# Chunk 0's four first-layer blocks in one piece, and raw weights loaded behind a read: one reordering at the start of a spectral network

## The chip, the cores and the metric

The kernel runs on one core of a Trainium2 chip. Its engines are PE (TensorE, with PEld for its weight loads), DVE (VectorE), ACT (ScalarE), POOL (GpSimd) and SP (SyncE, which here only issues DMAs). Each engine runs its own instructions strictly in order and waits on semaphores for the others. The metric is the device time of one execution in microseconds, the median of several runs.

## The reference

`x` has 4096 rows of 640 columns, everything in float32. A modulation vector made from `c` gives six vectors of 640.

```python
mod = (_silu(c) @ w_mod).reshape(c.shape[0], 6, 1, -1)      # sa, ca, ga, sb, cb, gb
h = _layernorm(x, axis=-1) * (1 + ca) + sa
x = x + ga * _A_ref(h, A_w1, A_b1, A_w2, A_b2)              # first network
h = _layernorm(x, axis=-1) * (1 + cb) + sb
x = x + gb * _B_ref(h, B_w_gate, B_w_up, B_w_down)          # second network (gated, 1728 wide)
```

The first network takes a real Fourier transform over the 4096 rows, cuts the 640 columns into 4 blocks of 160, and runs on each a two-layer complex network:

```python
hr = zr @ w1[0] - zi @ w1[1] + b1[0];  hi = zi @ w1[0] + zr @ w1[1] + b1[1]   # then relu
or_ = hr @ w2[0] - hi @ w2[1] + b2[0]; oi_ = hi @ w2[0] + hr @ w2[1] + b2[1]
```

The results are shrunk towards zero by 0.01 and transformed back.

## The kernel before

Products keep float32 precision by splitting: a value is rounded to a short format (its high part), and the rest (its low part) is a second operand, so that most products are made of three matmuls. `weights_high` and `weights_low` (L279, L285) do so for the weights: `w1a`, `w1b`, `w1c` of the first layer and `w2a`, `w2b`, `w2c` of the second. High parts are made on ACT or POOL (L283, L281), low parts on DVE (L286).

**The transform's first half.** `x` lies in SBUF as 8 tiles `xa`, tile 0 to 7. Each is normalised, multiplied by `fa` (L421, and for tiles 6 and 7 L437 in another cut of columns), copied back by ACT or DVE (`evac_c`, L449, L447), and written to DRAM, `s1`, by `write_s1` (L351, L354), in three parts `f`. Part 0 holds the frequencies that chunks 0 and 1 need. For tiles 6 and 7 part 0 is written in two pieces, named by their columns: `first` (0 to 127 and 512 to 639) and `rest` (128 to 511).

**Chunks.** There are 8 chunks of 256 frequencies. `load_g` (L310) reads a chunk's rows back from `s1` as tile `g`; chunk 0 comes in two halves, and the second half by `first` and `rest` again. `stage_b(ch, t)` (L613) is the transform's second half for one of five column tiles: t = 0 to 3 hold 128 columns of each block, and t = 4 the last 32 of all four. `evac_b` (L620 ACT, L621 DVE) makes `z` from t < 4. For t = 4 of chunk 0, `evac_r(0, b)` (L643 ACT, L653 DVE) makes the part `rz` of block b straight from PSUM. For every later chunk, `rem_high` and `rem_low` (L663 ACT, L667 DVE) make `rt`, `rem_move` (L676) writes it to DRAM (`rzd`), and `rem_read` (L682) reads it back rearranged as `rz`. For chunk 1 both are issued on POOL's queue, for later chunks on SP's.

**Blocks.** `stage_l1(ch, b)` (L708) is the first layer of one block: 21 matmuls on `z` and `rz`, three PSUM tiles `pl`, then `h` (L725, L726 ACT, L727 DVE) and `u` (L736 ACT, L737 DVE). `tail_l1` (L744 ACT, L745 DVE) makes `r` from `u`. `stage_l2(ch, b)` (L765) is the second layer: 16 matmuls on `h` and `r`, and an addition into `tt` (L767 DVE). A PSUM tile of the first two kinds of `pl` has two buffers, so a block's products wait for the `h` of the block before.

**Order.** It is written out by hand. A loop over positions p = 4 ch + b issues the first layer of block p, the `stage_b` that later positions need, the second layer of block p - 1, and the shrinking and back transform of older blocks. `idle(n)` puts n small products whose result nobody reads. On SP's queue all DMAs go out in the written order, and one that waits holds those behind it.

Of the kernel before, what the change touches and what calls it, by code (L numbers as in the profile page):

```python
# [171 lines left out]
def body(tc, x, w1, b1, w2, b2, wg, wu, wd, c, wm, k_fa, k_tb, k_tx, k_bm, k_bx, k_ga, k_ge, k_id, out, dbg=None):  # L172
    nc = tc.nc
    pe, act, dve, pool = nc.tensor, nc.scalar, nc.vector, nc.gpsimd
# [27 lines left out]
    with ExitStack() as top:  # L202
# [34 lines left out]
        with ExitStack() as af:  # L237
# [11 lines left out]
            def load_weights(pl, w, nm):  # L249
                rm = pl.tile([P, 2, NB, BS], F32, tag="rm", name=f"rm{nm}")  # L250
                rr = pl.tile([P, 2, NB, BS], F32, tag="rr", name=f"rr{nm}")
                nc.sync.dma_start(rm, w[0])
                nc.sync.dma_start(rr, w[1])
                return rm, rr
# [24 lines left out]
            def weights_high(w, h, l, v, sg, eng=None):  # L279
                if eng:  # L280
                    eng.tensor_scalar(w[:, :, h], v, sg, None, op0=OP.mult)  # L281
                else:
                    act.activation(w[:, :, h], v, AF.Copy if isinstance(sg, float) else AF.Identity, scale=sg)  # L283

            def weights_low(w, h, l, v, sg):  # L285
                dve.scalar_tensor_tensor(w[:, :, l], v, sg, f32(w[:, :, h]), op0=OP.mult, op1=OP.subtract)  # L286
# [15 lines left out]
            def load_g(ch, lo=0, hi=32, dma=None, cols=(slice(0, D),)):  # L302
                if ch < 4:
                    src = s1[ch // 2].rearrange("(c q j) n d -> c q n j d", c=2, q=4)[ch % 2]
                else:
                    src = s1[2].rearrange("(c q j f) n d -> f c q n j d", c=2, q=4, f=2)[ch // 2 - 2, ch % 2]
                if lo == 0:
                    gs[ch] = fx.tile([P, 4, D], F32, tag="gx", bufs=2, name=f"g{ch}")
                for e in cols:
                    (dma or nc.sync).dma_start(gs[ch][4 * lo:4 * hi, :, e], src[:, lo:hi, :, e].rearrange("q n j d -> n q j d"))  # L310
# [14 lines left out]
            def idle(n):  # L325
                pz = ps.tile([P, P], F32, tag="p2", name="pz")
                for _ in range(n):
                    mm(pz, ones, ones, start=True, stop=True)
# [4 lines left out]
            with tc.tile_pool(name="sp", bufs=1) as sp:  # L333
# [14 lines left out]
                def write_s1(t, f, cols=None, dma=None):  # L348
                    r = slice((0, 2, 1)[f], 128, (4, 4, 2)[f])
                    if t < 6:  # L350
                        (dma or nc.sync).dma_start(s1[f][:, 4 * t:4 * t + 4, :], xas[t][r])  # L351
                        return
                    for e in cols or (slice(0, 512), slice(512, 640)):
                        (dma or nc.sync).dma_start(s1[f][:, 4 * t:4 * t + 4, e], rst[t][r] if e.start == 512 else xas[t][r, :, e])  # L354
# [85 lines left out]
                def evac_c(t, i, eng=None):  # L440
                    if i == 4:
                        o = rst[t] = low_p.tile([P, 4, 128], F32, tag="e", bufs=2, name=f"rst{t}")
                    else:
                        o = xas[t][:, :, 128 * i:128 * i + 128]
                    v = pas[t, i].rearrange("p (a e) -> p a e", a=4)
                    if eng:
                        eng.tensor_copy(o, v)  # L447
                    else:
                        act.activation(o, v, AF.Copy)  # L449
# [23 lines left out]
                rest = (slice(128, 512),)  # L473
                write_s1(6, 0, first)
                write_s1(7, 0, first)
                load_g(0, 16, 32, None, first)
                for q in ((6, 2), (6, 3), (7, 1), (7, 2), (7, 3)):
                    dft_c(*q)
                jobs = prep_weights(raws[1], w1a, w1b, w1c, True)
# [2 lines left out]
                    weights_high(*job)  # L482
                evac_c(6, 2)
                evac_c(6, 3)
                evac_c(7, 1)
                for job in jobs[3:6]:
                    weights_high(*job)
# [1 line left out]
                evac_c(7, 3)  # L489
                for job in jobs[6:]:  # L490
                    weights_high(*job)
                write_s1(6, 0, rest)
                write_s1(7, 0, rest)
                raws[2] = load_weights(rp, w2, "2")
                load_g(0, 16, 32, None, rest)
                for t in (2, 3):
                    for f in (1, 2):
                        write_s1(t, f)
# [1 line left out]
                first_scale(3, 5)  # L500
                remainders(acc0, wx0)
                pm1 = columns(acc0, wx0)
                idle(8)
                for job in jobs[:4]:
                    weights_low(*job)
                dve.tensor_scalar(ca1, pm1[:, 0:5], 1.0, None, op0=OP.add)
# [26 lines left out]
            w2c = p2.tile([P, NB, 640], F32R, name="w2c")  # L533
            prep2 = prep_weights(raws[2], w2a, w2b, w2c, False)
            prep2 = [prep2[k] for k in (0, 3, 1, 4, 2, 5)]
            for n, job in enumerate(prep2):
                if n // 2 != 1:
                    weights_high(*job, pool)
            pool.dma_start(bm.rearrange("p a b c -> p (a b c)"), k_bm)


# [65 lines left out]
            def stage_b(ch, t):  # L607
                g, tb = gs[ch], tbs[ch]
                pb = (ps.tile([P, 2, 256], F32, tag="p2", name=f"pb{ch}_{t}") if (ch, t) in ((0, 1), (0, 3)) else
                      bank0(1 if t == 4 else 0, [P, 2, 256], f"pb{ch}_{t}"))  # L610
                col = slice(128 * t, 128 * t + 128)
                for j in range(4):
                    mm(pb[:, :, 64 * j:64 * j + 64], g[:, j, col], tb[:, j, :], start=True, stop=True)  # L613
                pbs[ch, t] = pb

            def evac_b(ch, t):
                pb = pbs[ch, t]
                z = lp.tile([P, 2, 2, 258], F32R, tag="z", bufs=4, name=f"z{ch}_{t}")
                zs[ch, t] = z
                act.activation(z[:, 0, :, 0:256], pb, AF.Identity, scale=ca1[:, t:t + 1])  # L620
                dve.scalar_tensor_tensor(z[:, 1, :, 0:256], pb, ca1[:, t:t + 1],  # L621
                                         f32(z[:, 0, :, 0:256]), op0=OP.mult, op1=OP.subtract)
                if ch == CE:
                    pool.tensor_copy(z[:, 0, :, 0:257:256], f32(edge[:, 0, t]))
                    pool.tensor_copy(z[:, 1, :, 0:257:256], f32(edge[:, 1, t]))
                    pool.tensor_copy(z[:, :, :, 257], zero[:, 0, 0])


            def evac_r(ch, b, part=None):
                if part != 1:  # L630
                    evac_rh(ch, b)
                if part != 0:
                    evac_rl(ch, b)
# [246 lines left out]
            for p in range(LAST + 1):  # L880
                ch, b = p // 4, p % 4
                on(shrink, p - 6)
                on(stage_l1, p)

                if p < 2:
                    todo = ([(0, 1), (0, 2)], [(0, 3), (1, 4), (1, 0)])[p]
                elif b == 0:
                    todo = [(ch, 3)]
                else:
                    todo = [(ch + 1, 4)] * (b == 1) + [(ch + 1, b - 1)]  # L890
                todo = [q for q in todo if q[0] < NCH]
                for q in todo:
                    stage_b(*q)
                    if q[1] < 4:
                        evac_b(*q)
                        if q[0] == 0:
                            evac_r(*q)
                for f, *a in sums.get(p, ()):
                    f(*a)
                if p == 0:  # L900
                    for job in prep2[2:4]:
                        weights_high(*job)

                if p == 1:
                    for job in prep2[3:]:
                        weights_low(*job)
                if b == 1 and ch + 1 < NCH:
                    rem_high(ch + 1)
                on(tail_l1, p)
                on(shrink_high, p - 6)  # L910
                if b == 1 and ch + 1 < NCH:
                    rem_low(ch + 1)
                    rem_move(ch + 1)
                if b == 2 and ch + 1 < NCH:
                    rem_read(ch + 1)
                on(stage_l2, p - 1)
                on(stage_i, p - 7)
                on(shrink_low, p - 6)
                if p < LAST:
                    on(shrink_parts, p - 5)  # L920
                if b == 0 and ch:
                    for i in range(4):
                        move_x(ch - 1, i)
                if p == 0:
                    for job in prep2[:3]:
                        weights_low(*job)
                if b == 3 and 2 < ch + 2 < NCH:
                    load_g(ch + 2)
                    load_tb(ch + 2)
                for f, *a in mods.get(p, ()):  # L930
                    f(*a)
                if p == LAST - 4:
                    cf += [rp.tile([P, 2, D], F32, tag=tag, name=f"cf{tag}") for tag in ("rm", "rr")]
                    load_first_rows(rb + 16, rl, nc.sync)
                elif p == LAST - 1:
                    load_first_rows(0, rb - 16, nc.sync)
# [1544 lines left out]
```

## Time and profile before

| what | value |
|---|---|
| median of 3 runs | 1466.28 us (1464.79 to 1469.08) |
| the profiled execution | 1463.59 us |
| its span, first to last instruction | 1461.8 us |
| granted TensorE clock, mean | 0.994 |
| busy: PE, PEld | 1411.0 (97%), 1333.6 (91%) us |
| busy: DVE, ACT, POOL | 1086.9 (74%), 783.2 (54%), 550.3 (38%) us |
| DMA | 380.05 MB, mean 260 GB/s |

A row of the timeline gives the start in us, the length, engine, line and operation, what it writes and reads, the shape and how many instructions it merges; in brackets stand the idle time of the engine just ahead of it and what ended that. A row on SPq or POOLq is the issue of a DMA, not its transfer. PE makes one float32 product in several passes, so a row can count more than the program has. The first products on `z` start near 54 us; the change lies between 46 and 98 us.

### The profile page before, as it was taken

The page shows a single profiled execution, that of the slowest core. Times are in us where ns is not written, and L with a number is a line of the kernel's source. Part 1 is how long each engine was busy: PE and PEld are TensorE (multiplying, and loading weights), DVE is VectorE, ACT ScalarE, POOL GpSimd, SP SyncE. Part 2 cuts the span into 40 slices and gives each one's busy share as a digit, 9 for nine tenths or more (in the row PEclk, how much of TensorE's full clock was granted, in tenths as well). Part 3 has the DMA queues.
Part 4 walks back from the last instruction along what each step waited for, and adds up shares of the span by engine and source line. Part 5 has one row for each costly group of instructions (what it writes and reads, how often), then busy time and mean ns, then how long its engine had stood idle before and what let it go on. Part 6 is the DMA issues. An engine that isn't in the chain of part 4 may idle for free.

```text
span 1461.8 us, 23933 instructions
## 1 busy us (share of the span) xinstructions
PE 1411.0 (97%) x8520; PEld 1333.6 (91%) x8520; DVE 1086.9 (74%) x1967; ACT 783.2 (54%) x1552; POOL 550.3 (38%) x645
## 2 busy tenths in 40 slices
PE   7789999988999999999999999999999999999998
PEld 2589999966888888899999999999999999999998
DVE  8748777867887798757887768787747767567775
ACT  7748888744544555545565546555425445245432
POOL 5300100044563454313445424444324545146533
PEclk9989999999999999999999999999999999999999
DMA  9877767638767988798977998877696666966552
GB/s 376 308 240 226 237 192 226 220 120 280 254 233 250 369 298 265 273 369 307 324 262 250 347 358 265 307 245 254 228 343 219 229 207 240 358 206 240 204 183 88
DMA packets 186474, 380.05 MB, mean 260 GB/s; under 512 B 22227, under 2 KB 104083, under 8 KB 184563
## 3 DMA queue, kind: packets, MB, share of 16 engines
q1 hardware_dynamic: 177826, 361.09, 71.9%
q0 software_dynamic: 6944, 14.82, 3.4%
q10 hardware_dynamic: 1584, 2.62, 0.5%
q8 instruction: 67, 1.10, 0.3%
q14 instruction: 53, 0.43, 0.1%
HBM read 263.91 MB, written 105.39 MB: 253 GB/s over the span
## 4 chain that ended last, share of the span: by engine, by line
PE 60%; DVE 8%; DMA 4%; issue 2%; ACT 1%; POOL 1%; SPq 0%; POOLq 0%; ACTq 0%; DVEq 0%
PE pd L2349 12%; PE pw L2028 8%; PE pw L2030 8%; PE pw L2029 8%; PE pd_X L2209 4%; DMA cr<-s 2%; PE pg L1892 2%; PE pg L1893 2%; PE pg L1894 2%; PE pd_Y L2209 2%; PE pw L2039 2%; PE pw L2040 2%; PE pw L2041 2%; DVE wb L1346 2%; PE pd_Z L2209 1%
## 5 line engine op out<-in xcount | busy, mean ns | idle before, releaser
L2349 PE MATMUL pd<-wdh,a 128*128 128x320 f32 x1040 | 239.2, 310 | 1.5 <-DVE x L2321 0.8
L2349 PEld LDWEIGHTS pd<-wdh,a 128*128 128x128 f32 x1040 | 176.2, 188 | 2.8 <-DVE x L2321 1.0
L1346 DVE TENSOR_TENSOR wb<-r,wb 128x512 fp32r<-128x512 f32 (+3 forms) x156 | 161.1, 1040 | 17.5 <-ACT wb L1343 15.5
L2349 PE MATMUL pd<-wdl,a 128*128 128x320 f32 x540 | 166.2, 309 | 0.0
L2028 PE MATMUL pw<-h,wt 128*128 128x384 f32 x416 | 140.7, 338 | 2.6 <-ACT s_x L2047 1.5
L2030 PE MATMUL pw<-h,wt 128*128 128x384 f32 x416 | 140.0, 337 | 0.0
L2029 PE MATMUL pw<-h,wt 128*128 128x384 f32 x416 | 139.5, 335 | 0.0
L2321 DVE TENSOR_TENSOR x<-x,pd 128x320 f32<-128x320 f32 x240 | 108.7, 477 | 37.7 <-PE pd L2349 34.1
L1343 ACT ACTIVATE wb<-r 128x512 fp32r<-128x512 f32 (+3 forms) x172 | 117.8, 703 | 33.8 <-PE pw L2041 24.3
L2030 PE MATMUL pw<-h,wb 128*128 128x384 f32 x312 | 104.8, 336 | 2.3 <-DVE wb L1346 2.3
L2028 PE MATMUL pw<-h,wb 128*128 128x384 f32 x312 | 105.1, 337 | 0.0
L2029 PE MATMUL pw<-h,wb 128*128 128x384 f32 x312 | 104.6, 335 | 0.0
L1892 PE MATMUL pg<-ht,wb 128*128 128x512 f32 x260 | 103.2, 397 | 1.3 <-ACT wb L1343 1.3
L1894 PE MATMUL pg<-ht,wb 128*128 128x512 f32 x260 | 101.9, 392 | 2.3 <-DVE wb L1346 2.3
L1893 PE MATMUL pg<-ht,wb 128*128 128x512 f32 x260 | 101.9, 392 | 0.0
L2349 PEld LDWEIGHTS pd<-wdl,a 128*128 128x128 f32 x540 | 101.4, 188 | 0.5
L2047 ACT ACTIVATE s_x<-pw 128x384 f32<-128x384 f32 x52 | 25.4, 489 | 114.0 <-PE pw L2030 113.3
L1605 POOL TENSOR_TENSOR cr<-cr,gab 128x640 f32<-128x640 f32 x28 | 47.9, 1710 | 100.9 <-DMA cr<-s 96.3
L2028 PEld LDWEIGHTS pw<-h,wt 128*128 128x128 f32 x416 | 78.1, 188 | 4.5 <-ACT s_x L2047 2.4
L822 POOL DMA_DIRECT2D s<-co x28 | 15.9, 568 | 165.6 <-ACT co L821 157.8
L2029 PEld LDWEIGHTS pw<-h,wt 128*128 128x128 f32 x416 | 78.2, 188 | 0.0
L2030 PEld LDWEIGHTS pw<-h,wt 128*128 128x128 f32 x416 | 78.1, 188 | 0.0
(335 smaller groups left out, 4064.8 us busy)
## 6 DMA issues: line engine op xcount, KB each, us to landing
wt<-td SPq DMA_DIRECT2D x104, 512.0 KB, 5.3
hs<-ho SPq DMA_DIRECT2D x52, 512.0 KB, 5.1
h<-hs SPq DMA_DIRECT2D x32, 768.0 KB, 8.4
r<-in_B_w_gate_dram SPq DMA_DIRECT2D x36, 640.0 KB, 5.0
r<-in_B_w_up_dram SPq DMA_DIRECT2D x36, 640.0 KB, 5.3
wdr<-wdd SPq DMA_DIRECT2D x21, 640.0 KB, 5.2
td<-wt SPq DMA_DIRECT2D x25, 512.0 KB, 5.5
g<-s SPq DMA_DIRECT2D x7, 1280.0 KB, 9.1
```

Source lines behind the costliest of these rows:

```text
L1343: act.activation(wbs[t, n][:, 0, ks, e], raw[t, n][:, ks, e], AF.Copy)
L1346: (pool if onp else dve).tensor_tensor(wbs[t, n][:, 1, ks, e], raw[t, n][:, ks, e], f32(wbs[t, n][:, 0, ks, e]), op=OP.subtract)
L1605: pool.tensor_tensor(crs[r], crs[r], gab, op=OP.mult)
L1892: mm(b, wh, hh, start=(kk == 0), stop=False)
L1893: mm(b, wh, hl, start=False, stop=False)
L1894: mm(b, wl, hh, start=False, stop=(kk == 4))
L2028: mm(b, w(0, kp), a[:, kp, 0], start=start and kp == 0, stop=False, skip_group_check=not start)
L2029: mm(b, w(0, kp), a[:, kp, 1], start=False, stop=False, skip_group_check=not start)
L2030: mm(b, w(1, kp), a[:, kp, 0], start=False, stop=kp == 1, skip_group_check=not start)
L2209: mm(bk[b, i][:, :320], x, y, start=new and j == 0, stop=j == len(seq) - 1, skip_group_check=not new)
L2321: dve.tensor_tensor(x2[:, e], x2[:, e], x[0][:, :320], op=OP.add)
L2349: mm(pd[g, hf][0][:, :320], l, m, start=i == 0, stop=i == len(s) - 1 and not (last and len(gs) > 1))
```

## The change

In the start of chunk 0 the order is changed on every engine; behind it nothing is changed but the numbering of buffers and lines.

- All four first-layer blocks of chunk 0, with the `stage_b` and the tails that they need, stand in one piece at p = 0. Chunk 1's first `stage_b` (t = 4 and 0) and the second layer of block 0 stand behind the fourth block. Before, they stood behind the second block.
- The six low parts of the second layer's weights stand together on DVE behind the fourth block. Before, three stood behind the first block, and three behind the second.
- All six high parts are made on POOL. Before, `w2b` was made on ACT.
- On SP, the `rest` piece of tile 6 goes out ahead of the first read of chunk 0's second half, and the raw weights of the second layer (`rm`, `rr`) behind its second read instead of ahead of it.
- `idle(8)` becomes `idle(6)`.

```diff
                 write_s1(7, 0, first)
-                load_g(0, 16, 32, None, first)
                 for q in ((6, 2), (6, 3), (7, 1), (7, 2), (7, 3)):
                     dft_c(*q)
...
                 evac_c(6, 2)
                 evac_c(6, 3)
+                write_s1(6, 0, rest)
+                load_g(0, 16, 32, None, first)
                 evac_c(7, 1)
...
-                write_s1(6, 0, rest)
                 write_s1(7, 0, rest)
+                load_g(0, 16, 32, None, rest)
                 raws[2] = load_weights(rp, w2, "2")
-                load_g(0, 16, 32, None, rest)
...
-                idle(8)
+                idle(6)
...
-            for n, job in enumerate(prep2):
-                if n // 2 != 1:
-                    weights_high(*job, pool)
+            for job in prep2:
+                weights_high(*job, pool)
...
             for p in range(LAST + 1):
                 ch, b = p // 4, p % 4
                 on(shrink, p - 6)
-                on(stage_l1, p)
-
-                if p < 2:
-                    todo = ([(0, 1), (0, 2)], [(0, 3), (1, 4), (1, 0)])[p]
+                if p > 3:
+                    on(stage_l1, p)
+
+                if p == 0:
+                    for q in range(4):
+                        stage_l1(0, q)
+                        for t in ((1, 2), (3,), (), ())[q]:
+                            stage_b(0, t)
+                            evac_b(0, t)
+                            evac_r(0, t)
+                        tail_l1(0, q)
+                    for job in prep2:
+                        weights_low(*job)
+                    continue
                 elif b == 0:
...
-                        if q[0] == 0:
-                            evac_r(*q)
...
-                if p == 0:
-                    for job in prep2[2:4]:
-                        weights_high(*job)
-
-                if p == 1:
-                    for job in prep2[3:]:
-                        weights_low(*job)
...
-                on(tail_l1, p)
+                if p > 3:
+                    on(tail_l1, p)
...
-                if p == 0:
-                    for job in prep2[:3]:
-                        weights_low(*job)
```

SP's queue around the second half of chunk 0 (`s10` is part 0 of the DRAM array, `xa6` and `xa7` tiles 6 and 7, `g0` chunk 0, `rm2` and `rr2` the raw weights):

```order
 L354 DMA s10<-rst7_511 32x4x128
+L354 DMA s10<-xa6_270 32x4x384
 L310 DMA g0_447<-s10 64x4x128 x2
-L354 DMA s10<-xa6_270 32x4x384
 L354 DMA s10<-xa7_313 32x4x384
-L252 DMA rm2_548<-in_A_w2_dram 128x1280
-L253 DMA rr2_549<-in_A_w2_dram 128x1280
 L310 DMA g0_447<-s10 64x4x384
+L252 DMA rm2_549<-in_A_w2_dram 128x1280
+L253 DMA rr2_550<-in_A_w2_dram 128x1280
 L351 DMA s11<-xa2_124 32x2560
```

One write moved ahead of a read, and two loads of raw weights behind another.

PE before, from the third `stage_b` of chunk 0 (`pb` is named by chunk and t, `pl` and `pc` by chunk, block and part):

```order
L613 MATMUL pb0_3_768<-tb0_401,g0_447 128x2x64 x4
L613 MATMUL pb1_4_780<-tb1_594,g1_592 128x2x64 x4
L613 MATMUL pb1_0_785<-tb1_594,g1_592 128x2x64 x4
L765 MATMUL pc0_0_0_803<-w2a_627,h0_0_0_681 128x320 x3
L765 MATMUL pc0_0_0_803<-w2b_628,h0_0_1_688 128x320 x3
```

PE now, from the end of the fourth block:

```order
L707 MATMUL pl0_3_2_846<-z0_3_768,w1b_93 128x256 x2
L707 MATMUL pl0_3_2_846<-rz0_654,w1c_94 128x256
L612 MATMUL pb1_4_865<-tb1_592,g1_590 128x2x64 x4
L612 MATMUL pb1_0_870<-tb1_592,g1_590 128x2x64 x4
L764 MATMUL pc0_0_0_883<-w2a_625,h0_0_0_681 128x320 x3
```

Chunk 1's two `stage_b` and the second layer's first block moved behind the third and the fourth first-layer block.

DVE before, from the tail of the first block (`r2_0_0` is `r` of chunk 0, block 0; `rt1` the part of chunk 1 that goes through DRAM):

```order
L745 SCALAR_TENSOR_TENSOR r2_0_0_695<-u1_0_0_694,r2_0_0_695 64x256
L286 SCALAR_TENSOR_TENSOR w2a_627<-rm2_548,w2a_627 128x4x160 x2
L286 SCALAR_TENSOR_TENSOR w2b_628<-rm2_548,w2b_628 128x4x160
L727 TENSOR_TENSOR h0_1_0_740<-h32_0_1_0_739,h0_1_0_740 128x256
L727 TENSOR_TENSOR h0_1_1_753<-h32_0_1_1_752,h0_1_1_753 128x256
L737 SCALAR_TENSOR_TENSOR u1_0_1_764<-pl0_1_2_757,b1r_85,u0_0_1_763 64x256
L621 SCALAR_TENSOR_TENSOR z0_3_773<-pb0_3_768,ca1_71,z0_3_773 128x2x256
L653 SCALAR_TENSOR_TENSOR rz0_654<-pb0_4_646,ca1_71,rz0_654 32x256 x2
L621 SCALAR_TENSOR_TENSOR z1_0_790<-pb1_0_785,ca1_71,z1_0_790 128x2x256
L286 SCALAR_TENSOR_TENSOR w2b_628<-rm2_548,w2b_628 128x4x160
L286 SCALAR_TENSOR_TENSOR w2c_629<-rr2_549,sgn_77,w2c_629 128x4x160
L286 SCALAR_TENSOR_TENSOR w2c_629<-rr2_549,w2c_629 128x4x160
```

DVE now, from the tail of the fourth block:

```order
L744 SCALAR_TENSOR_TENSOR r2_0_3_854<-u1_0_3_853,r2_0_3_854 64x256
L286 SCALAR_TENSOR_TENSOR w2a_625<-rm2_549,w2a_625 128x4x160 x2
L286 SCALAR_TENSOR_TENSOR w2b_626<-rm2_549,w2b_626 128x4x160 x2
L286 SCALAR_TENSOR_TENSOR w2c_627<-rr2_550,sgn_77,w2c_627 128x4x160
L286 SCALAR_TENSOR_TENSOR w2c_627<-rr2_550,w2c_627 128x4x160
L620 SCALAR_TENSOR_TENSOR z1_0_875<-pb1_0_870,ca1_71,z1_0_875 128x2x256
L666 SCALAR_TENSOR_TENSOR rt1_878<-pb1_4_865,ca1_71,rt1_878 128x2x256
```

The six low parts are in one piece, behind all four blocks' own work and ahead of chunk 1's.

## The prediction

> **What bounds the kernel now.** I read the page first, then busy time by stage, then the timeline of each engine where TensorE is not full. Times are us from the span's start.
>
> ```profile
> span 1461.8 us, 23933 instructions
> ...
> PE   7789999988999999999999999999999999999998
> ```
>
> ```profile
> 84.00:98.00 14.00, 12.70 (x93) 12.49 (x91) 6.75 (x14) 6.09 (x14) 2.25 (x4) 0.93 0.86 241
> 98.00:200.00 102.00, 101.95 (x795) 101.60 (x796) 77.60 (x147) 83.49 (x172) 9.88 (x28) 1.00 0.70 209
> ```
>
> Columns are the stretch, its length, busy time of PE, PEld, DVE, ACT and POOL, granted clock, DMA share, GB/s. From 98 to 200, PE is busy 101.95 of 102 at clock 1.00: there only its own work sets the pace. The order of every engine behind this place is unchanged. So whatever the edit does must show up as the moment at which PE enters that full stretch, and it is handed to the end one for one: the later thin slices of the page's PE row hold waits between engines that move along with PE. The holes ahead of it are these:
>
> ```profile
> 56.98 0.75 PE L708 MATMUL pl<-rz,w1c 128*128 128x256 f32 x5
> ...
> 61.09 2.87 PE L613 MATMUL pb<-tb,g 128*128 128x128 f32 x16 [3.36 <-DMA g<-s]
> ...
> 73.81 3.76 PE L613 MATMUL pb<-tb,g 128*128 128x128 f32 x16 [5.58 <-DVE rz L653]
> ...
> 87.65 0.68 PE L765 MATMUL pc<-w2a,h 128*128 128x320 f32 x3
> ...
> 90.08 0.52 PE L708 MATMUL pl<-z,w1a 128*128 128x256 f32 x3
> ...
> 92.58 1.06 PE L613 MATMUL pb<-tb,g 128*128 128x128 f32 x8
> 93.39 0.69 PE L765 MATMUL pc<-w2a,h 128*128 128x320 f32 x3
> ...
> 98.05 0.47 PE L708 MATMUL pl<-rz,w1c 128*128 128x256 f32 x2 [1.35 <-DMA rz<-rzd]
> ```
>
> PE waits 3.36 for the second part of `g0`, 5.58 for `evac_r(0, 3)` to free the bank that chunk 1 needs, and 1.35 for `rz` of chunk 1, which goes to DRAM and back. The last of these waits is the door into the full stretch. The rows in between give prices at full clock: a second-layer block takes 90.08 - 87.65 = 2.43, a first-layer block 92.58 - 90.08 = 2.50, a `stage_b` 93.39 - 92.58 = 0.81.
>
> **The second part's read.** On SP, the queue of nearly all loads:
>
> ```profile
> 46.39 0.58 SPq L354 DMA_DIRECT2D s<-rst  x1
> 49.71 1.26 SPq L310 DMA_DIRECT2D g<-s  x2
> 51.06 1.27 SPq L354 DMA_DIRECT2D s<-xa  x2
> 52.39 0.59 SPq L252 DMA_DIRECT2D rm<-in_A_w_dram  x1
> ...
> 54.42 0.58 SPq L310 DMA_DIRECT2D g<-s  x1
> ...
> 58.12 1.17 SPq L310 DMA_DIRECT2D g<-s  x1
> ...
> 68.92 0.31 SPq L515 DMA_DIRECT2D s1h<-g  x1
> ```
>
> ```profile
> g<-s SPq DMA_DIRECT2D x2, 1280.0 KB, 10.3
> ...
> rm<-in_A_w_dram SPq DMA_DIRECT2D x1, 640.0 KB, 4.8
> ...
> rzd<-rt POOLq DMA_DIRECT2D x1, 512.0 KB, 6.8
> rz<-rzd POOLq DMA_DIRECT2D x4, 128.0 KB, 6.0
> s<-xa SPq DMA_DIRECT2D x2, 192.0 KB, 2.6
> ```
>
> The second fence is the table of DMA issues from 36 to 110; its last figure is the median from issue to landing. Tile 6's write fits into SP's free time between 46.97 and 49.71, so the first read stays at 49.71, tile 7's write goes out at 50.97 and lands 2.6 later at 53.6, and the read of columns 128 to 511 is issued at 53.6 instead of 54.42, with no raw weights ahead of it. It now takes 61.09 - 54.42 = 6.67. The ends for the new latency are the 2.6 of the 192 KB writes and that 6.67; between the 192 KB and 640 KB rows, 384 KB interpolate to 3.5, which I take: it lands at 57.1. The first block's products end at 56.98 + 0.75 = 57.73, so the 3.36 goes. What is late next is the evacuation, below.
>
> The raw weights leave 2 later (54.2 against 52.39) and stand behind the read. POOL's work on them:
>
> ```profile
> 57.39 3.71 POOL L281 TENSOR_SCALAR w2a<-rm 128x640 fp32r<-128x640 f32 x2 [16.12 <-PE pl L708]
> ...
> 83.15 0.77 POOL L676 DMA_DIRECT2D rzd<-rt  x1 [12.24 <-DVE tt L767]
> 90.56 2.25 POOL L682 DMA_DIRECT2D rz<-rzd  x4 [6.64 <-PE pc L765]
> ```
>
> The 57.39 is the landing of `rm` (52.39 + 4.8). It becomes about 59.5, and six instructions of 1.9 instead of four end near 71.5. VectorE asks for the last at 76.5 (below), so this is hidden with some 5 to spare. Chunk 1's `g1` landed by 68.92; the stream of loads is held back some 0.9 (SP has nothing to send while it waits for tile 7's write), so 69.8. PE asks for it behind the fourth block, near 70.7 (ACT needs 2 for `h` and `u` of that block, rows below, and ends its `r` at 73.1): hidden, by 1.
>
> **Four blocks in a row.** PE has 2.50 of work per block, but each needs ScalarE:
>
> ```profile
> 59.01 0.38 ACT L736 ACTIVATE u<-pl 64x256 f32<-64x256 f32 x1
> ...
> 67.23 0.40 ACT L744 ACTIVATE r<-u 64x256 fp32r<-64x256 f32 x1
> 67.65 0.47 ACT L725 ACTIVATE h<-pl,b1m 128x256 f32<-128x256 f32 x1
> ...
> 69.25 0.38 ACT L736 ACTIVATE u<-pl 64x256 f32<-64x256 f32 x1
> 69.65 0.69 ACT L620 ACTIVATE z<-pb,ca 128x512 fp32r<-128x512 f32 x1
> 70.36 0.95 ACT L643 ACTIVATE rz<-pb,ca 32x256 fp32r<-32x256 f32 x2
> ```
>
> From `r` at 67.23 to the end of `rz` at 71.31 one block costs ACT 4.08, more than PE's 2.50. ACT is free of the first block at 59.39 and has three blocks and one `r` to go: 59.39 + 3 x 4.08 + 0.42 = 72.05. Waits for VectorE inside (`r` needs its `u`, the second `rz` its predecessor) I put at 1.1: `r` of the fourth block at 73.1, VectorE's half at 73.5. The two `w2b` that ACT loses are work it no longer has.
>
> VectorE's order is shown with the change: all six low parts of the second layer's weights now stand behind the fourth block's `r`, and `z1_0` and `rt1` of chunk 1 behind them; before, three stood behind the first block and three ahead of `rt1`, with two blocks done.
>
> ```profile
> 79.72 0.88 DVE L286 SCALAR_TENSOR_TENSOR w2c<-rr,sgn,w2c 128x640 fp32r<-128x640 f32 x1
> 80.52 0.82 DVE L286 SCALAR_TENSOR_TENSOR w2c<-rr,w2c 128x640 fp32r<-128x640 f32 x1
> ...
> 81.80 0.75 DVE L667 SCALAR_TENSOR_TENSOR rt<-pb,ca,rt 128x512 fp32r<-128x512 f32 x1
> ```
>
> Six at 0.77 from start to start: 73.5 + 4.6 = 78.1, then `z1_0` and `rt1` end at 79.6, against 81.80 + 0.75 = 82.55. That term is **-2.9**. Ends: -4 if ACT never waits, +1 if the second read lands as late as its old latency makes it (60.3 instead of 57.1, so ACT starts 2.1 later) and PE runs cold for the blocks (1.7).
>
> **The door.** `rt1` goes out at 83.15, its reads at 90.56, the product starts at 98.05: 15.5 from the end of `rt1`. By the same rows it would now start at 79.6 + 15.5 = 95.1. PE gets there far sooner: the second layer's first block ends near 80 (`w2c` at 78.1, then half a block), and two `stage_b`, two second-layer blocks and the start of the next take 2 x 0.81 + 2 x 2.43 + 0.7 = 7.2, some 8 with a cold start: 88, against 96.7. So 8 of lead turn into a wait of 7 or more: the holes are not filled but moved to one place. The reads, 7.49 from issue to use, ran partly after the big loads had landed (stretch 84 to 98: DMA share 0.86). Three earlier, they share the engines with `g2` longer. Ends: 0, and (2.25 of issuing + 10.3, the landing of a 1280 KB load) - 7.49 = +5.1. I take **+1.0**, near the first, as POOL's 512 KB write landed in 6.8 in a full stretch.
>
> The Trainium skill, page "DMA: Bandwidth & Descriptors", section "Queues, rings and completion order", says that each DMA engine takes turns between queues packet by packet. By it POOL's reads would not stand behind SP's loads and the 1.0 would go towards 0, the sum to -0.8; the trace agrees so far (6.8 against 10.3).
>
> ```profile
> 74.00:76.00 2.00, 2.00 (x10) 2.00 (x11) 0.00 (x0) 0.00 (x0) 0.00 (x0) 0.50 0.93 339
> 76.00:78.00 2.00, 2.00 (x11) 2.00 (x10) 0.00 (x0) 0.40 (x1) 0.00 (x0) 0.50 1.03 423
> 78.00:80.00 2.00, 1.04 (x5) 0.64 (x4) 1.68 (x3) 1.16 (x3) 0.00 (x0) 0.71 0.99 410
> ```
>
> After the 5.58 wait PE ran at half clock from 73.81 to 78 at least: 4.2 x 0.5 = 2.1 lost, up to 2.7 with the next row. After the 1.35 wait it lost nothing (98 to 200 at 1.00). A wait of 7 puts the door in the first class: **+2.1**.
>
> The Trainium skill, page "TensorE: Matmul & The Clock Gate", Part 1, says that an idle window of about 3.4 us halves the clock until another such window has been busy. By that alone the loss is 1.7, an estimate, and the sum 0.4 lower; the trace agrees with the half.
>
> The two dropped `idle` products end at 52.3 beside the first read's landing (49.71 + 2.6): nothing, at most 0.3.
>
> Sum: -2.9 + 1.0 + 2.1 = +0.2. On the profiled execution (1463.59, the span and 1.8 around it) that is 1463.8; on the median, 2.7 above it, 1466.5. A measurement of this kernel tells about 0.3%, 4.4 us, from no change. The terms' ends give the likeliest case its own range: 1463.5 to 1470.
>
> **Rivals.** *POOL's round trip stretches* (slower). The write and reads of `rz` now lie wholly under SP's writes of tiles 0, 4 to 7 and `g2`. Against: the write's 6.8 in a full stretch. For: loads there land in 10.3. If both took that, 3.5 + 5.1 = 8.6 in place of 1.0; halfway 5.8 gives -2.9 + 5.8 + 2.1 = +5, 1471.5, at the end 1474. It decides once the product that now starts at 98.05 starts later than 100.4 (4.4 - 2.1 = 2.3 later, with the cold clock).
>
> *The round trip shrinks* (faster). With 4.8 of `rm` as landing for write and reads it is 2.0 + 1.2 shorter: -2.9 - 3.2 + 2.1 = -4.0, with an early `rt1` -5.1: 1461. Against it: fewer idle DMA engines than before, not more.
>
> *The edit doesn't do what it says*: the second read lands at 60.3 all the same. Then ACT starts 2.1 later: +2.3, 1468.6, still inside 0.3%.
>
> **How the numbers follow.** Forecast 0.45, the late read 0.12, the stretched trip 0.28, the shrunk trip 0.15. Faster by over 0.3% is the shrunk trip, 0.15; slower the stretched one, 0.28; the rest 0.57. The range from 1461 to 1472.5 cuts about half of the fast case and the upper third of the slow one.
>
> **What would show it.** In the changed profile: no wait of PE on `g` near 58; ACT nearly full from 59 to 73; `rt` ending near 79.6; one wait of PE on `rz` of 6 to 9 with half clock behind it, its product starting near 96. It is wrong if that wait is short or missing, if `rt` ends after 82.5, or if PE is not full from there on.

## The result and the profile after

The changed kernel took 1466.31 us (median of 12 runs, 1461.72 to 1472.49), the kernel before 1465.13 in the same comparison (12 runs, 1460.85 to 1470.58). The ratio is 1.0008, with a 95% interval of 0.9990 to 1.0025: no change that can be told. The forecast was 1466.5, from a median of 1466.28 before (3 runs) and a change of +0.2.

The profiled execution took 1462.63, with a span of 1460.8.

The windows at the door and behind it (columns as in the prediction: stretch, length, busy time of PE, PEld, DVE, ACT and POOL, clock, DMA share, GB/s):

```profile
84.00:98.00 14.00, 6.21 (x44) 6.04 (x43) 3.22 (x6) 0.69 (x1) 2.25 (x4) 0.83 0.84 238
98.00:200.00 102.00, 102.00 (x791) 101.62 (x789) 77.33 (x146) 83.08 (x170) 9.75 (x28) 0.99 0.70 208
```

Of the 14 us ahead of 98, PE was busy in 12.70 before and is busy in 6.21 now. The stretch behind it is as full as it was (102.00 against 101.95). PE's timeline shows where its waits went:

```profile
51.94 2.02 PE L612 MATMUL pb<-tb,g 128*128 128x128 f32 x16 [0.54 <-DMA g<-s]
...
57.62 2.05 PE L612 MATMUL pb<-tb,g 128*128 128x128 f32 x16 [0.36 <-DMA g<-s]
...
75.72 0.41 PE L764 MATMUL pc<-w2a,h 128*128 128x320 f32 x1 [2.74 <-DVE w2a L286]
...
97.28 0.77 PE L707 MATMUL pl<-rz,w1c 128*128 128x256 f32 x2 [7.79 <-DMA rz<-rzd]
...
100.42 1.05 PE L612 MATMUL pb<-tb,g 128*128 128x128 f32 x8
```

The 3.36 on `g` is 0.36, the 5.58 on `rz` of chunk 0 is gone, 2.74 on `w2a` is new, and the 1.35 at the door is 7.79. What feeds the door, from ACT's and DVE's timelines of after (the last row of a block, the first low part, `rt1`):

```profile
73.20 0.42 ACT L743 ACTIVATE r<-u 64x256 fp32r<-64x256 f32 x1 [0.54 <-DVE u L736]
...
74.10 1.56 DVE L286 SCALAR_TENSOR_TENSOR w2a<-rm,w2a 128x640 fp32r<-128x640 f32 x2
...
79.24 0.74 DVE L666 SCALAR_TENSOR_TENSOR rt<-pb,ca,rt 128x512 fp32r<-128x512 f32 x1
```

POOL's timeline (its last work on the raw weights, the write and the reads of the trip):

```profile
68.70 1.81 POOL L281 TENSOR_SCALAR w2c<-rr 128x640 fp32r<-128x640 f32 x1
...
80.29 0.77 POOL L675 DMA_DIRECT2D rzd<-rt  x1 [8.62 <-DVE rt L666]
87.71 2.25 POOL L681 DMA_DIRECT2D rz<-rzd  x4 [6.65 <-PE pc L764]
```

SP's timeline (the second part's read of `g0`, and `g2`):

```profile
53.23 0.55 SPq L310 DMA_DIRECT2D g<-s  x1
...
82.64 1.32 SPq L310 DMA_DIRECT2D g<-s  x1
```

and SP's issue of `g2` in the kernel before:

```profile
82.71 1.26 SPq L310 DMA_DIRECT2D g<-s  x1
```

From the table of DMA issues of after between 36 and 110 (KB each, median us from issue to landing):

```profile
rzd<-rt POOLq DMA_DIRECT2D x1, 512.0 KB, 6.8
rz<-rzd POOLq DMA_DIRECT2D x4, 128.0 KB, 8.0
...
g<-s SPq DMA_DIRECT2D x1, 384.0 KB, 4.4
```

`rt1` ends at 79.98 (82.55 before), so the write leaves 2.86 earlier, and the reads too (87.71 against 90.56). But the reads need 8.0 to land where they needed 6.0, and the product on `rz` starts at 97.28 instead of 98.05. Most of what was won ahead of the door is given back in front of it. SP's issue of `g2`, 1280 KB, did not move (82.64 against 82.71): the reads that leave earlier meet more of it.

In all that follows, **lag** is the time from PE's first `stage_b` of chunk 0 to the first `stage_b` behind the door, chunk 1's third. Here it is 100.42 - 51.94 = 48.48; before it was 99.91 - 52.41 = 47.50, from PE's timeline:

```profile
52.41 2.02 PE L613 MATMUL pb<-tb,g 128*128 128x128 f32 x16
...
99.91 1.05 PE L613 MATMUL pb<-tb,g 128*128 128x128 f32 x8
```

By this the edit cost 0.98. That is read from one profile of each kernel. Three of the runs below (ACT's queue, the filled wait, `g2` behind the reads) have the same order on PE, ACT and DVE up to the end of `rt1` as the changed kernel. From the first `stage_b` to that end the four executions take 27.55, 27.55, 28.00 and 28.04, so a difference of 0.5 between two profiles says nothing. The 0.98 stays put over the full stretch. The same product in PE's timeline of before:

```profile
197.45 1.05 PE L613 MATMUL pb<-tb,g 128*128 128x128 f32 x8
```

and of after:

```profile
197.93 1.05 PE L612 MATMUL pb<-tb,g 128*128 128x128 f32 x8
```

They stand 0.48 apart, and the first `stage_b` stood 0.47 the other way. Behind 280 the two executions drift by some us in either direction, and the span of after ends 1.0 shorter. So single times differ by more than the edit does, and the lag is what the runs below are judged by, with times of several rounds where these exist.

### The profile page after: what moved, and what is told of

The parts are those of the page before. It is cut to its first block, busy times and chain, and to the rows that moved or that the text cites. A ratio compares the mean times of both kernels' runs of the same rounds, so it can differ in the third digit from the quotient of the medians.

```text
span 1460.8 us, 23921 instructions
## 1 busy us (share of the span) xinstructions
PE 1408.0 (96%) x8516; PEld 1331.2 (91%) x8516; DVE 1081.5 (74%) x1967; ACT 782.2 (54%) x1550; POOL 551.3 (38%) x647
## 4 chain that ended last, share of the span: by engine, by line
PE 59%; DVE 8%; DMA 6%; issue 2%; ACT 2%; POOL 1%; SPq 0%; POOLq 0%; ACTq 0%; DVEq 0%
PE pd L2347 12%; PE pw L2026 7%; PE pw L2028 7%; PE pw L2027 7%; PE pd_X L2207 4%; DMA cr<-s 3%; PE pg L1890 2%; PE pg L1891 2%; PE pd_Y L2207 2%; PE pg L1892 2%; PE pw L2037 2%; PE pw L2038 2%; PE pw L2039 2%; DVE wb L1344 2%; PE pd_Z L2207 1%
```

## The experiments

The theory on record for the first runs: the door is the end of `rt1` plus the trip of `rz` to DRAM and back, 15.5 to 17.3, and what stands behind the door is then paid at half clock. What came to it on the way is that the trip is no constant: its reads share the DMA engines with SP's big loads and take longer among them. Against this stand three others: POOL's queue is the slow part, and another queue would do better; the half clock alone explains the loss; the order of the blocks costs PE time by itself.

### Chunk 1's remainder ahead of the low parts

Chunk 1's two `stage_b`, `rt1` and its write stand ahead of the six low parts:

```diff
                         tail_l1(0, q)
+                    stage_b(1, 4)
+                    rem_high(1)
+                    rem_low(1)
+                    rem_move(1)
+                    stage_b(1, 0)
+                    evac_b(1, 0)
                     for job in prep2:
                         weights_low(*job)
```

The same steps at the next block are dropped.

> The changed kernel, but with rt of chunk 1 made and sent off ahead of the six low parts of the second layer's weights. My theory (the door is the end of rt plus the trip through DRAM): rt ends near 75.1 instead of 79.98, the trip takes 15.5 to 17.3, so the first product on rz starts at 90.6 to 92.4 instead of 97.28. TensorE comes there near 90.8 (its second layer waits 1.5 longer for the weights), waits 0 to 1.6 and stays at full clock. Chunk 1's stage_b for t = 3, which stands behind that product and started 47.50 after the first stage_b before and 48.48 after, starts 41 to 42.5 after it. Time near 1460, ratio to before 0.995 to 0.997. Rival (the wait on rz only hides the next one, on weights or evacuation): less than 2 us better than the changed kernel, with another wait of TensorE in its place.

PE's timeline of this run (the wait for the weights, the door's product, the `stage_b` behind it):

```profile
76.73 0.64 PE L764 MATMUL pc<-w2a,h 128*128 128x320 f32 x1 [3.89 <-DVE w2a L286]
...
91.03 0.40 PE L707 MATMUL pl<-rz,w1c 128*128 128x256 f32 x2
...
92.81 1.05 PE L612 MATMUL pb<-tb,g 128*128 128x128 f32 x8
```

POOL's and SP's timelines (write and reads of the trip, then `g2`):

```profile
74.86 0.77 POOL L675 DMA_DIRECT2D rzd<-rt  x1 [2.64 <-DVE rt L666]
81.42 2.24 POOL L681 DMA_DIRECT2D rz<-rzd  x4 [5.80 <-DMA rzd<-rt]
...
83.54 0.85 SPq L310 DMA_DIRECT2D g<-s  x1
```

and the DMA issues (KB each, median us to landing):

```profile
rz<-rzd POOLq DMA_DIRECT2D x4, 128.0 KB, 6.2
```

The reads leave at 81.42, ahead of `g2` at 83.54, and PE does not wait at the door at all: no bracket on the 91.03. The lag is 92.81 - 51.83 = 40.98, 6.5 less than before. One part of the expectation failed: the clock did not stay full. PE waited 3.89 for `w2a`, and ran at half clock from 75.4 to 85.6; even so it reached the door only after `rz` was there. Time: 1461.20 (12 runs) against 1465.53 (17), ratio 0.9968, interval 0.9949 to 0.9987: 4.7 us faster by the ratio. So the trip is what set the door in the changed kernel, and the order of the four blocks is no hindrance.

### ACT's queue for the trip

The change with the write and the reads of chunk 1's `rz` on ACT's queue instead of POOL's:

```diff
-                (pool if ch == 1 else nc.sync).dma_start(rzd[ch, ...
+                (nc.scalar if ch == 1 else nc.sync).dma_start(rzd[ch, ...
```

(and the same for the reads).

> The changed kernel, with the trip of chunk 1's rz (one write, four reads) issued from ScalarE's queue instead of POOL's. If the trip is long because the 16 DMA engines are full of SP's writes and loads, it stays at 15 to 18 from the end of rt to the product, which starts at 95 to 98. If POOL's way of issuing is what is slow, the trip falls to 11 to 13 and the product starts near 92.

ACT's and PE's timelines of this run:

```profile
85.38 0.58 ACTq L675 DMA_DIRECT2D rzd<-rt  x1
86.00 0.69 ACT L619 ACTIVATE z<-pb,ca 128x512 fp32r<-128x512 f32 x1 [11.53 <-DMA s<-xa]
...
98.25 0.56 PE L707 MATMUL pl<-rz,w1c 128*128 128x256 f32 x2 [4.94 <-DMA rz<-rzd]
```

and its DMA issues:

```profile
rz<-rzd ACTq DMA_DIRECT2D x4, 128.0 KB, 2.7
```

`rt1` ended at 79.54, but the write left at 85.38: ACT stood idle for 11.53 until one of SP's DMAs landed, as the profile infers it. So the run tests less than it was meant to. The reads then left at 93.89 and landed in 2.7. The door stands at 98.25 again, with another queue, a write 5 later and reads 6 later: POOL's queue as the cause gets no support, but the queue alone was not isolated. The trip, 18.7, lies outside both of the expected ranges, and the lag is 49.40, more than with the change alone. One time, 1467.19.

### A filled wait

The change with 28 filler products of PE ahead of the door's block:

```diff
+                if p == 4:
+                    idle(28)
                 if p > 3:
                     on(stage_l1, p)
```

> The changed kernel, with 28 small products that nobody reads (about 7 us) ahead of chunk 1's first first-layer block, so that TensorE does not stand idle while rz is on its way. My theory (the wait is the same, but the clock falls in it): the first product on rz still starts near 97.3, the clock stays at 1.00 behind it, and chunk 1's stage_b for t = 3 starts near 47.2 after the first stage_b instead of 48.48, so 1.3 us less. Rival (the clock costs nothing here): no difference within 0.2, or later by what the added products take.

PE's timeline of this run at the door:

```profile
97.81 0.48 PE L707 MATMUL pl<-rz,w1c 128*128 128x256 f32 x2 [1.65 <-DMA rz<-rzd]
...
99.67 1.05 PE L612 MATMUL pb<-tb,g 128*128 128x128 f32 x8
```

The door is where it was, the clock behind it is full, and the lag is 99.67 - 52.87 = 46.80, 1.68 less than with the change alone. Not all of that is the clock: from the door's product to the `stage_b` PE now takes 1.86 instead of 3.14, which is 1.28, and the other 0.4 arose ahead of the door and lies within the scatter of 0.5. So the half clock behind the door costs 1.28 here. It does not explain where the door stands, so it is only a part of the story. One time, 1464.92.

### The parts of the change by themselves

The kernel before with only the moves on SP's queue (the first hunks of the diff), and the change without them:

> The kernel before, with only SP's part of the change (tile 6's write ahead of the first read, raw weights behind the second). My theory: TensorE's wait on g falls from 3.36 to under 1, rt ends 2.5 to 2.9 earlier (near 79.8), the trip takes 15.5 to 17.3, and the wait on rz grows from 1.35 to between 2 and 4. Chunk 1's stage_b for t = 3 starts 45 to 47.5 after the first stage_b instead of 47.50: 0 to 2.5 us gained. Rival (each wait is paid by itself): the whole 3 us are gained and the wait on rz stays near 1.35.

> The changed kernel, with SP's part of the change undone (tile 6's write behind the first read, raw weights ahead of the second; four blocks in one piece). My theory: TensorE waits about 3.4 for g again, ScalarE starts its three blocks 2 to 2.9 later, rt ends near 82 to 83, the trip takes 15.5 to 17.3 and the wait on rz stays near 8 with half clock behind it: chunk 1's stage_b for t = 3 starts 50 to 51.5 after the first stage_b (47.51 before, 48.48 after). Rival (the blocks gain by themselves, and the raw weights' move is what costs): 47.5 or less.

PE's timeline with SP's part alone:

```profile
57.59 2.05 PE L613 MATMUL pb<-tb,g 128*128 128x128 f32 x16 [0.55 <-DMA g<-s]
...
71.13 3.76 PE L613 MATMUL pb<-tb,g 128*128 128x128 f32 x16 [6.61 <-DVE rz L653]
...
96.96 0.47 PE L708 MATMUL pl<-rz,w1c 128*128 128x256 f32 x2 [3.05 <-DMA rz<-rzd]
```

PE's and POOL's timelines with the blocks alone:

```profile
61.02 3.49 PE L612 MATMUL pb<-tb,g 128*128 128x128 f32 x16 [3.70 <-DMA g<-s]
...
97.77 0.77 PE L707 MATMUL pl<-rz,w1c 128*128 128x256 f32 x2 [5.44 <-DMA rz<-rzd]
...
93.04 2.24 POOL L681 DMA_DIRECT2D rz<-rzd  x4 [8.55 <-DMA rzd<-rt]
```

and the DMA issues with the blocks alone:

```profile
rz<-rzd POOLq DMA_DIRECT2D x4, 128.0 KB, 2.9
```

SP's part does what it says: the wait on `g` falls from 3.36 to 0.55, and most of it comes back as 6.61 on `rz` and 3.05 at the door. Lag 47.10, 0.4 less than before, which is too little to tell. The blocks alone give 49.12, 1.6 more than before, and less than the 50 to 51.5 that were expected: the wait at the door was 5.44 instead of about 8, and the trip 14.4, below its range. Over the three kernels `rt1` ended at 79.88, 79.98 and 83.41, but the door stood at 96.96, 97.28 and 97.77. An `rt1` 3.4 later moved it by 0.5: its reads, issued at 93.04, behind the big loads, took 2.9 instead of 8.0. This is what showed that the trip is no constant. The comparison isn't clean, since with the blocks alone SP's loads also ended sooner (`g2` was issued at 81.16, and the DMA share is 0.12 from 92 to 93, against 1.13 after). Times: 1464.96 and 1468.43, one each; the changed kernel's own times spread from 1461.72 to 1472.49, so a single time tells nothing of 2 us.

### The kernel before with `rt1` ahead of its low parts

Three of the low parts at the second block are moved behind `rt1`'s evacuation and write, in the kernel before:

```diff
-                if p == 1:
-                    for job in prep2[3:]:
-                        weights_low(*job)
...
                     rem_move(ch + 1)
+                if p == 1:
+                    for job in prep2[3:]:
+                        weights_low(*job)
```

> The kernel before, with rt of chunk 1 made and sent off ahead of the three low parts that stood in front of it, and nothing else. My theory: rt ends about 2.4 earlier (near 80.1), the trip takes 15.5 to 17.3, rz is there at 95.6 to 97.4, TensorE comes there near 97 as its second layer gets the weights 0.7 later: the wait on rz falls from 1.35 to under 0.7, and chunk 1's stage_b for t = 3 starts 46.7 to 47.4 after the first stage_b instead of 47.51. So on the kernel before this move is worth under 1 us, as TensorE itself is late there. Rival (the trip alone sets the door there too): 45 or less.

PE's timeline of this run, in the second layer's first block:

```profile
81.67 0.63 PE L765 MATMUL pc<-w2b,h 128*128 128x320 f32 x1 [2.87 <-DVE w2b L286]
```

A miss: lag 48.62, more than before. PE waits 2.87, and then 0.63, for the low parts that were moved, runs at half clock from 81.1 to 87.9, and so reaches the door at 98.92, later than the reads (97.16). The wait at the door is gone because PE is late, not because the trip got short. `rt1` itself came 1.7 sooner (80.88), and its reads landed 0.75 sooner. One time, 1463.32.

### The first experiment with fillers

14 fillers behind chunk 1's `evac_b`, so that PE would not lose its clock in the wait of 3.89 on `w2a`:

```diff
                     evac_b(1, 0)
+                    idle(14)
                     for job in prep2:
```

> The first experiment (rt ahead of the six low parts) with 14 small products that nobody reads (3.5 us) between chunk 1's stage_b for t = 0 and the second layer's first block, where TensorE waits 3.9 for the low parts. My theory of the clock: no half clock from 75 to 86 there (10.2 us of it without these products), so TensorE reaches the product on rz 2.5 to 3.5 earlier and now waits for it until about 90; chunk 1's stage_b for t = 3 starts 39 to 40.5 after the first stage_b instead of 40.98. Rival (the clock is not lost through that wait): 40.9 to 41.5.

PE's timeline of this run (the first wait on the low parts, and the door):

```profile
77.31 0.41 PE L764 MATMUL pc<-w2a,h 128*128 128x320 f32 x1 [1.16 <-DVE w2a L286]
...
95.04 0.47 PE L707 MATMUL pl<-rz,w1c 128*128 128x256 f32 x2 [3.47 <-DMA rz<-rzd]
```

POOL's and SP's timelines (the reads, and `g2`):

```profile
83.38 2.24 POOL L681 DMA_DIRECT2D rz<-rzd  x4 [7.17 <-PE pc L764]
...
83.26 1.37 SPq L310 DMA_DIRECT2D g<-s  x1
```

and the DMA issues:

```profile
rz<-rzd POOLq DMA_DIRECT2D x4, 128.0 KB, 8.3
```

Another miss, and the most telling run: lag 45.60. The clock still halved from 78.9 to 85.7, in spite of the fillers, behind waits of 1.16 and 0.76 on the low parts; a third, of 0.71, lies inside the spell. And the write took 7.3 (6.0 in the first experiment), so the reads left at 83.38, 0.12 behind `g2` instead of 2.1 ahead of it. (The profile puts the wait of the reads down to PE, but here as in before, after and the first experiment they left 0.6 behind the landing of the write.) They took 8.3 instead of 6.2, and the door came to 95.04 instead of 91.03 or earlier. `rt1` had ended 0.6 later than in the first experiment; the door moved by 4. Against after, `rt1` ended 4.9 earlier and the door came 2.2 earlier: behind `g2`, less than half of the gain arrives. One time, 1460.07.

### `g2` behind the reads

What is claimed of `g2` is tried directly. The change with the load of `g2` taken from SP's queue and put on POOL's behind the reads, `tb2` behind it on SP:

```diff
-            load_g(2)
-            load_tb(2)
...
+                if p == 2:
+                    load_g(2, dma=pool)
+                    load_tb(2)
```

> The changed kernel, with the 1280 KB load of chunk 2 issued on POOL's queue behind the four reads of rz instead of on SP's ahead of them. If the reads took 9.6 instead of 7.5 because they share the DMA engines with that load, the trip falls from 17.3 to between 13.5 and 15.5 and the product on rz starts at 93.5 to 95.5. If POOL's own way of issuing and moving is what takes the time, the trip stays at 16.5 to 17.5.

PE's and POOL's timelines of this run (the door, the `stage_b` behind it, and the reads):

```profile
93.58 0.48 PE L705 MATMUL pl<-rz,w1c 128*128 128x256 f32 x2 [3.55 <-DMA rz<-rzd]
...
96.55 1.49 PE L610 MATMUL pb<-tb,g 128*128 128x128 f32 x8
...
87.82 2.25 POOL L679 DMA_DIRECT2D rz<-rzd  x4 [6.37 <-DMA rzd<-rt]
```

and its DMA issues:

```profile
rz<-rzd POOLq DMA_DIRECT2D x4, 128.0 KB, 4.0
```

The reads leave at 87.82, as with the change (87.71), from the same queue, and land in 4.0 instead of 8.0. From the end of `rt1` (80.37) the trip takes 13.2 instead of 17.3, and the lag 44.18, 4.3 less, although the clock was halved behind the door here too. The queue is the same in both, so what stretched the reads is SP's load, and not POOL's queue by itself. `g2`, 1280 KB, is by far the largest piece of what moved; the 256 KB of `tb2` went from 84.00 to 86.21 with it and was not tried alone. The loads behind `g2` on SP count too: after, `g2` itself had landed by 91.9, and the reads came in up to 97.1, together with 320 KB of `wm`, issued at 87.25 and landed at 97.2; with `g2` out of the way that piece of `wm` landed at 91.2. So `g2` holds up the stream as a whole, and its share is not parted from that of the loads behind it. At 13.2 the trip is a little under the 13.5 to 15.5 expected. One time, 1465.44, against 1463.51 of the kernel before on that chip: the gain of 3.3 against before doesn't show in it.

The same move in the kernel before:

> The kernel before, with the load of chunk 2 issued on POOL's queue behind the reads of rz (the edit of the eighth experiment), and nothing else. By what that run showed (the reads of rz share the engines with this load), they land by 93 to 95 instead of 97.9. But in the kernel before TensorE itself comes to the product only at 96.7: the wait on rz (1.35) goes to 0 and no more is gained, so chunk 1's stage_b for t = 3 starts 46.0 to 46.4 after the first stage_b instead of 47.51. Rival (the trip sets the door in the kernel before, as in the changed one): 44.5 or less.

PE's timeline of this run (a wait of the second layer, and the door's product):

```profile
79.93 0.41 PE L763 MATMUL pc<-w2b,h 128*128 128x320 f32 x1 [1.56 <-DVE w2b L286]
...
97.75 0.40 PE L706 MATMUL pl<-rz,w1c 128*128 128x256 f32 x2
```

and its DMA issues:

```profile
rz<-rzd POOLq DMA_DIRECT2D x4, 128.0 KB, 3.0
```

The trip shrinks here as well: the reads take 3.0 instead of 6.0, and the door's product has no wait. But the lag is 47.61, as before (47.50), not the 46 that was expected. PE's waits in the second layer's first block came to 1.56 and 0.97, and it ran at half clock from 80.6 to 87.4, one spell of 3.4 longer than in before (82.6 to 86.0); so it reached the door only then. In the kernel before, PE's own work ahead of the door is nearly as late as the trip. The same edit is worth 4.3 in the changed kernel and nothing here: with the change the trip alone holds the door. One time, 1465.35.

Last, the first experiment with that move:

> The changed kernel with both edits: rt of chunk 1 ahead of the six low parts, and chunk 2's load behind the reads of rz. The reads go out near 81.5 and land by 87 to 88.5 instead of 89.5 in the first experiment. As TensorE came to the product at 91.03 there without a wait, nothing more is gained at this place: chunk 1's stage_b for t = 3 starts 40.3 to 41.3 after the first stage_b (40.98 there), and the ratio to before is 0.9945 to 0.998. Rival (the trip still holds TensorE up in the first experiment): 39.5 or less. If chunk 2's load, now some 8 later, comes too late, TensorE waits for g near 97 and the gain shrinks by that wait.

PE's timeline of this run, the `stage_b` behind the door:

```profile
92.78 1.05 PE L610 MATMUL pb<-tb,g 128*128 128x128 f32 x8
```

Lag 92.78 - 52.06 = 40.72, no wait at the door, as in the first experiment; its reads had left ahead of `g2` already, so the move adds nothing of size. Time: 1458.09 (11 runs) against 1464.66 (15), ratio 0.9961, interval 0.9946 to 0.9976: 6.6 us by the medians, 5.7 by the ratio. This is the shortest time here, though it was taken beside the kernel before only. That it beats the first experiment is not shown (0.9968, and the intervals overlap).

## Why the prediction was right, step by step

**The full stretch and the door.** Held: PE is full from the door on, and the change in lag carried unchanged to 200. That it is handed to the end one for one could not be seen in one profile each, as the executions drift by more; the two versions with a much shorter lag (6.5 and 6.8) came out 4.7 and 5.7 us faster, which is most of it.

**The read and the four blocks.** The second read was forecast to be issued at 53.6 and to land 3.5 later; it was issued at 53.23 and took 4.4. PE's wait fell from 3.36 to 0.36; it was forecast to go. ACT was nearly full to 73.20 + 0.42 = 73.62 (forecast 73.1), DVE's low parts began at 74.10, and `rt1` ended at 79.98 (forecast 79.6). Measured from the first `stage_b`, which came 0.47 sooner, `rt1` is 2.10 earlier, not 2.9: right in mechanism, 0.8 too large, of which up to 0.5 can be the scatter between executions. The two dropped fillers gained nothing: PE waited 0.54 on `g` in their place.

**The cover.** POOL's work on the raw weights ended at 70.5 (forecast 71.5), 3.6 ahead of DVE's first low part: hidden, as said. A wait of 2.74 on `w2a` ahead of the second layer was not forecast; it halved the clock from 76.25 to 83.1, and cost nothing since PE then waited 7.79 all the same.

**The trip.** Forecast +1.0, measured 17.30 - 15.50 = +1.8. The step behind it, that earlier reads share the engines longer with SP's loads, `g2` the largest, is shown (8.0 with `g2` ahead, 4.0 with it behind). The term was too small, and its form was wrong: the trip was taken as a constant with a surcharge. The windows of after show the load on the DMA engines fall off:

```profile
94.00:96.00 2.00, 0.00 (x0) 0.00 (x0) 0.00 (x0) 0.00 (x0) 0.00 (x0) 0.50 0.63 129
96.00:98.00 2.00, 0.72 (x3) 0.76 (x4) 0.00 (x0) 0.00 (x0) 0.00 (x0) 0.50 0.06 20
```

The share (last but one) is 0.63, then 0.06, and the door opens right there, at 97.28. The reads are themselves a part of this load. With them behind `g2`, the door stood between 96.96 and 98.05 in before, after, the filled wait and SP's part alone, with `rt1` ending between 79.88 and 82.55. It is no fixed time, though: reads that left sooner, at 83.38 and 81.42, gave 95.04 and no wait at 91.03. A sum from the reads' place in SP's stream of loads would have served better than one from the end of `rt1` alone.

The Trainium skill, page "DMA: Bandwidth & Descriptors", section "Queues, rings and completion order", has each DMA engine take turns between queues; the prediction drew from it that the trip would not grow (its -0.8). The trace does not agree with that use: reads from a queue of their own took twice as long with SP's load in flight.

**The half clock.** Forecast +2.1. From the product on `rz` to the next `stage_b` PE took 3.14 (1.86 before): +1.28, and the run that kept the clock has 1.86 there again. Right in sign and mechanism, too large by 0.8, as the spell, from 93.3 to 100.1, began in the wait and only its rest lay behind the door. The spells in the traces of before and after are 3.41 and 6.83 long. The Trainium skill, page "TensorE: Matmul & The Clock Gate", Part 1, has an idle window of about 3.4 us halve the clock until another has been busy; the estimate of 1.7 made from it was the closer one. But in the run with 14 fillers the clock fell with no idle stretch of that length ahead: the waits just before were 1.16 and 0.76.

The sum measured: -2.10 + 1.80 + 1.28 = +0.98, against +0.2 forecast. Three terms were off by 0.8 each, two of them against the third, so that the sum came out that close is in part luck. So is the 0.2 between 1466.5 and 1466.31: the forecast started from 1466.28, and the kernel before came to 1465.13 over 12 runs. Times cannot test the sum, since half the width of the interval is some 2.6 us, and any small sum would have looked the same; the profile does, and there the mechanism held: the holes were moved to one place in front of the door, the start of the trip came sooner and the trip grew longer.

**The rivals.** The stretched trip (slower) was right in its mechanism, but it was to decide only with the door's product behind 100.4, and that started at 97.28. By the forecast's own 95.1 that would have been a trip longer by 5.3; it grew by 1.8. (One figure of the prediction is off here: halfway between 1.0 and 8.6 lies 4.8 and not 5.8, which gives 1470.3 instead of 1471.5; nothing else hangs on it.) The shrunk trip did not come, and the late read did not either.

## What to carry to other kernels

Before pricing a step that ends in a DMA round trip, look at what big load is in flight when its reads go out: behind it they land late, and much of what was won further up is lost again (here 2.6 us at the end of `rt1` became 0.8 at the door). Then it pays to move the load or to get the reads out ahead of it, not to speed up what feeds them. And an edit that gathers several small waits into one long one should be charged for the half clock behind it (1.28 here).

## What the runs showed of the hardware

- Four reads of 128 KB on POOL's queue landed, by the median, in 2.9 when issued behind SP's burst of loads (the blocks alone), in 4.0 and 3.0 with `g2` out of it, in 6.0 and 6.4 when issued 7.9 and 6.4 behind `g2` (before, SP's part alone), and in 8.0, 7.9 and 8.3 when issued 5.1, 3.1 and 0.1 behind it (after, the filled wait, the first experiment with fillers).
- In one run a DMA on ACT's queue was issued only 5.8 after its data were there, and ACT's own work stood behind it. The profile puts the wait down to one of SP's DMAs; the cause was not tried.
- PE's clock halved not only after one long wait: with fillers ahead, waits of 1.16 and 0.76 within 2.7 stood ahead of a spell from 78.9 to 85.7, while the wait of 1.35 at the door of before cost nothing.
